# A decode layer on one core: the w2 product in two halves, its weights in runs of 5, 4, 3 and 1 rows, fewer tail DMAs

## The chip, the cores and the metric

The kernel runs on one core of a Trainium2 chip. The metric is the device time of one execution, in microseconds (us). One more number occurs, the *span*, which the profiler measures from the first to the last instruction of one execution; it is about 1.4 us shorter than the time. Engines: PE does matmuls, DVE (VectorE) and ACT (ScalarE) elementwise work, POOL (GpSimd) little here, SP issues loads. The loads run on 16 DMA engines.

Executions of the kernel before lie within about 0.3 us of 661.5 (661.31 to 661.86 in this study); those of some edited kernels spread over about 1 us.

## The reference

```python
h  = x + attention(layernorm(x), k_cache, v_cache, wq, wo)     # B=4, Sq=1, D=640, H=32, Sk=4096, Dh=128
h1 = layernorm(h) @ w1 + b1                                    # w1: 640 x 1728
act = h1 * tanh(softplus(h1))                                  # mish
out = h + act @ w2                                             # w2: 1728 x 640
```

The caches are 268 MB in bf16, the weights 15 MB. All must be read once.

## The kernel before

SP issues every load in order. A loop over 16 tiles of k and v takes the first 624 us. After the last k tile is folded, SP issues the weights of the tail: wo (six DMAs), w1 (three), the last 64 rows of w2 (the *remainder*, since 1728 = 13 x 128 + 64), then the 13 full row groups of w2 (four DMAs). A row group is called a "row" below: 128 rows of w2, one on each partition. Only where the DMAs of the remainder are counted ("eight DMAs of 8 rows") is a row a single row of w2.

```python
WOS = [(k, 0, G) for k in range(NHG - 1)] + [(NHG - 1, a, b) for a, b in ((0, 4), (4, 7), (7, G))]
W1S = (0, 2, DC - 1, DC)                  # w1 in pieces of 2, 2, 1 rows
W2S = tuple(range(0, FM, FI)) + (FM,)     # w2 in runs of 4, 4, 4, 1 rows
# ... cut: sync_prog
for k in range(FT // 8):                  # the remainder: eight DMAs of 8 rows
    r = slice(k // 4 * 32 + k % 4, k // 4 * 32 + 32, 4)
    load(sp, w2_tail[r, :], B_w2[FM * P : F, :][r, :], ("w2t", k), "WT")
sp.need(("PV", NT - 2))
for k, (j0, j1) in enumerate(zip(W2S, W2S[1:])):
    load(sp, w2_sb[:, j0:j1, :], ...)
```

On PE, the tail is one straight program. It adds h1 up as each piece of w1 lands, adds h to the output sum y2, runs four filler matmuls (`busy(4)`, products with zeros whose only use is to keep PE busy), waits for `act`, and adds the w2 rows. The sum y2 has 640 columns for 4 batch rows. It lies in four quarters of 160 columns on PSUM partitions 0, 32, 64, 96, so one w2 row is four matmuls.

```python
# ... cut: pe_tail
for c0, c1 in zip(W1S, W1S[1:]):
    if c1 == DC:
        ...                               # b1 is added before the last piece
    pe.need(("w1", c0))
    for j in [FM] + list(range(FM)):
        for c in range(c0, c1):
            wd = WD if c0 == 0 else 1     # WD = 16: 64 columns on the first piece, 4 on later ones
            mm(h1_w[..., j, 0:wd, :], w, cen[:, c, :]...to_broadcast([P, wd, N]), ...)
...                                       # h into y2: 40 bf16 matmuls (high and low part)
busy(4)
pe.need("act")
def w2_mm(j):
    for k in range(CG):                   # 4 quarters of OC = 160 columns
        mm(y2_ps[k * QD : k * QD + N, :], act[0:rows, j, :], w2_sb[:, j, cs], ...)
pe.need(("w2t", FT // 8 - 1)); w2_mm(FM)
for j0, j1 in zip(W2S, W2S[1:]):
    pe.need(("w2", j0))
    for j in range(j0, j1): w2_mm(j)
```

One DVE copy then takes y2 to SBUF, and four stores (two on the SP queue, two on the ACT queue) write it out.

The softmax here doesn't subtract the row's maximum and nothing guards it: scores larger than these inputs give would overflow.

## Time and profile before

| | before |
|---|---|
| time, median of 6 | 661.53 us (661.38 to 661.82) |
| span of the profiled execution | 660.0 us |
| load queue, share of 16 engines' span | 99.4% |
| PE / DVE busy | 58% / 62% |
| last w2 landing | 657.57 us |

The engine and queue parts of the profile's page, kernel before (busy us, share of the span, instructions; then packets, MB and share of the 16 engines' span):

```profile
PE 383.8 (58%) x2636; PEld 68.4 (10%) x1680; DVE 407.8 (62%) x257; ACT 40.7 (6%) x157; POOL 1.7 (0%) x12
q1 hardware_dynamic: 6912, 283.35, 99.4%
```

No compute engine is near full; the load queue is. The kernel is bound by reading 283 MB, and a change of the tail can only win what lies between the end of the loading and the end of the kernel, or shorten the last loads.

The end of the chain of waits, kernel before (start us, length us, what):

```profile
...
642.29 14.90 DMA slotA<-in_B_w_dram
657.19 0.04 issue
657.23 0.65 PE red L730 x20
657.89 0.02 issue
657.91 0.32 DVE o_bf L726
```

The chain runs through the load of w2 (slotA), then through the last five rows (20 matmuls), then through the copy. PE was waiting for w2.

The timeline of the same end (start, length, engine, line, operation, output<-input, shapes, count, and in brackets the idle time before it and what ended it):

```profile
652.03 0.71 PE L730 MATMUL red<-cen,slotB 128*64 128x4 bf16 x14
...
654.32 0.22 DVE L719 SCALAR_TENSOR_TENSOR act<-tb,hm 128x56 bf16<-128x56 f32 x1
...
654.90 0.30 PE L730 MATMUL red<-w_tail,act 64*4 64x160 bf16 x4
...
655.13 1.27 PE L730 MATMUL red<-slotA,act 128*4 128x160 bf16 x32
...
657.23 0.62 PE L730 MATMUL red<-slotA,act 128*4 128x160 bf16 x20 [0.83 <-DMA slotA<-in_B_w_dram]
657.91 0.32 DVE L726 CAST o_bf<-red 128x160 bf16<-128x160 f32 x1 [3.37 <-PE red L730]
658.26 0.65 SPq L263 DMA_DIRECT2D out_dram<-o_bf  x2
658.27 0.62 ACTq L263 DMA_DIRECT2D out_dram<-o_bf  x2
```

The last w1 matmuls end at 652.7, act is there at 654.5, and PE has 0.83 us of idle time before the last rows. Two stores of each queue take 0.65 us to issue.

### The profile page before, as it was taken

The numbers are of one execution on the slowest core, as the hardware profiler recorded it, in microseconds if no ns is written. First come the engines' busy times: TensorE is split into PE (matmuls) and PEld (weight loads), VectorE is DVE, ScalarE is ACT, GpSimd is POOL, SyncE is SP. The second block draws the span as 40 slices with busy tenths as digits, with TensorE's granted clock in tenths as the row PEclk, the third lists the DMA queues.
The fourth block names the chain that finished last, engine by engine and source line by source line (L and its number), as shares of the span: only waits on it lengthen the run. The fifth ranks groups of instructions, "written<-read, shape, count | busy, mean of one in ns | idle before, by whom it ended". The sixth has DMA issues, their size and how long they took to land. (4 is left out here: it accounts for less than half of the span.)

```text
span 660.0 us, 4989 instructions
## 1 busy us (share of the span) xinstructions
PE 383.8 (58%) x2636; PEld 68.4 (10%) x1680; DVE 407.8 (62%) x257; ACT 40.7 (6%) x157; POOL 1.7 (0%) x12
## 2 busy tenths in 40 slices
PE   1255758457327595838307395838434757665877
PEld 0000100101101010101100010000110001010145
DVE  1087988386048778677219798749206688957612
ACT  0200000000000000000000000000000000000011
POOL 0000000000000000000000000000000000000000
PEclk9778787879659796869668887879876769796868
DMA  9999999999999999999999999999999999999997
GB/s 418 409 445 445 438 441 417 422 441 438 438 437 425 429 437 437 441 437 421 433 437 437 441 437 417 437 437 433 441 441 417 437 433 437 441 441 417 425 416 312
DMA packets 6954, 283.50 MB, mean 430 GB/s; under 512 B 857, under 2 KB 1184, under 8 KB 2208
## 3 DMA queue, kind: packets, MB, share of 16 engines
q1 hardware_dynamic: 6912, 283.35, 99.4%
q8 instruction: 7, 0.11, 0.1%
q14 instruction: 3, 0.02, 0.0%
q10 hardware_dynamic: 32, 0.01, 0.0%
HBM read 283.35 MB, written 0.01 MB: 429 GB/s over the span
## 5 line engine op out<-in xcount | busy, mean ns | idle before, releaser
L529 DVE TENSOR_TENSOR slotA<-slotA,q_bc 128x8192 bf16<-128x8192 bf16 x32 | 140.7, 4416 | 93.1 <-DMA slotA<-in_A_k_cache_dram 93.1
L529 DVE TENSOR_TENSOR slotB<-slotB,q_bc 128x8192 bf16<-128x8192 bf16 x32 | 140.7, 4418 | 18.4 <-DMA slotB<-in_A_k_cache_dram 18.4
L540 DVE TENSOR_REDUCE s_f<-red 128x64 f32<-128x1024 f32 x64 | 78.0, 1219 | 96.3 <-PE red L740 96.2
L740 PE MATMUL red<-slotA,ident 128*128 128x512 bf16 x480 | 135.8, 446 | 0.0
L740 PE MATMUL red<-slotB,ident 128*128 128x512 bf16 x480 | 126.1, 422 | 0.0
L730 PE MATMUL red<-slotA,ident 128*128 128x512 bf16 x32 | 14.7, 458 | 129.4 <-PEq L49 129.4
L730 PE MATMUL pv<-slotC,e 128*32 128x512 bf16 x768 | 51.9, 430 | 37.3 <-PEq L49 34.3
L730 PE MATMUL red<-slotB,ident 128*128 128x512 bf16 x32 | 14.2, 443 | 89.1 <-PEq L49 89.1
L406 ACT ACTIVATE ex<-s_f 128x64 bf16<-128x64 f32 x64 | 16.4, 256 | 513.3 <-DVE s_f L540 513.3
L554 DVE TENSOR_TENSOR e<-ex,hmask 128x512 bf16<-128x512 bf16 x64 | 39.8, 684 | 0.0
L730 PEld LDWEIGHTS pv<-slotC,e 128*32 128x32 bf16 x768 | 22.1, 106 | 95.4 <-issue 81.3
L730 PEld LDWEIGHTS red<-slotA,ident 128*128 128x128 bf16 x32 | 3.2, 99 | 198.0 <-issue 197.9
L730 PEld LDWEIGHTS red<-slotB,ident 128*128 128x128 bf16 x32 | 3.1, 98 | 171.1 <-issue 171.1
L730 PEld LDWEIGHTS o_ps<-pv_sb,selo 128*32 128x32 f32 x136 | 13.5, 109 | 62.6 <-issue 62.6
L730 PE MATMUL o_ps<-pv_sb,selo 128*32 128x128 f32 x136 | 18.0, 276 | 0.0
L730 PE MATMUL pv<-slotA,e 128*32 128x512 bf16 x256 | 14.5, 380 | 0.6 <-PEq L49 0.5
L416 ACT COPY pv_sb<-pv 128x512 f32<-128x512 f32 x16 | 9.4, 586 | 69.5 <-PE pv L730 69.5
L406 ACT ACTIVATION_READ_ACCUMULATOR ex<-s_f 128x1 f32 x64 | 11.9, 186 | 0.0
L730 PEld LDWEIGHTS pv<-slotA,e 128*32 128x32 bf16 x256 | 6.9, 97 | 23.6 <-issue 17.8
L579 DVE RECIPROCAL rl<-misc 32x1 f32<-32x1 f32 x4 | 0.6, 150 | 12.6 <-PE misc L730 12.6
L519 DVE CAST b1T<-pv 128x13 bf16<-128x13 f32 x1 | 0.2, 174 | 12.1 <-PE pv L730 12.1
L730 PE MATMUL y_ps<-a_t,slotB 128*128 128x64 bf16 x160 | 7.3, 211 | 0.0
(107 smaller groups left out, 69.2 us busy)
## 6 DMA issues: line engine op xcount, KB each, us to landing
slotC<-in_A_v_cache_dram SPq DMA_DIRECT2D x2, 4096.0 KB, 42.2
slotC<-in_A_wq_dram SPq DMA_DIRECT2D x1, 5120.0 KB, 15.4
slotB<-in_A_wo_dram SPq DMA_DIRECT2D x3, 1280.0 KB, 15.4
slotA<-in_B_w_dram SPq DMA_DIRECT2D x3, 640.0 KB, 13.9
slotB<-in_B_w_dram SPq DMA_DIRECT2D x2, 864.0 KB, 22.1
slotB<-in_A_wo_dram SPq DMA_DIRECT2D x1, 640.0 KB, 19.0
slotB<-in_A_wo_dram SPq DMA_DIRECT2D x1, 480.0 KB, 19.8
slotB<-in_B_w_dram SPq DMA_DIRECT2D x1, 432.0 KB, 22.8
```

The source lines that it names most:

```text
L406: lambda: a.activation(out=ex[:, sl], in_=s_f[:, sl], func=ACT.Exp, scale=SCALE, accum_out=rs[:, b, s : s + 1],),
L416: lambda: a.copy(out=pv_sb[:, :, :].rearrange("p r d -> p (r d)"), in_=pv[:, :]),
L519: dv.do(lambda: v.tensor_copy(out=b1T[:, 0:FM], in_=b1_ps[:, 0:FM]), "b1m", DV)
L529: lambda: v.tensor_tensor(out=t, in0=t, in1=q_bc[:, hg, b, :].unsqueeze(1).to_broadcast([P, RS, Dh]), op=ALU.mult,),
L540: lambda: v.tensor_reduce(out=s_f[:, s * RS : (s + 1) * RS], in_=red[:, k : k + 2, :].rearrange("p k (r c) -> p (k r) c", c=CW), axis=AX.X ...
L554: lambda: v.tensor_tensor(out=e[:, sl, :], in0=ex[:, sl].unsqueeze(2).to_broadcast([P, RS, G]), in1=hmask[:, :].unsqueeze(1).to_broadcast( ...
L579: dv.do(lambda: v.reciprocal(out=rl[:, :], in_=l_ps), ("rl", hg), DV)
L730: lambda: nc.tensor.matmul(out_, lhsT=lhsT, rhs=rhs, start=start, stop=stop, skip_group_check=skip),
L740: return t.add_instruction(mybir.InstMatmult(name=nc.get_next_instruction_name(), engine=mybir.EngineType.PE, ins=[t.lower_ap(rhs), t.lowe ...
```

## The change

The intent reads from the diff: fewer and larger tail DMAs, two output halves with two copies side by side and one store a queue, and matmuls arranged to keep PE's clock up.

```diff
-    FI = 4
+    FR = (5, 4, 3, 1)                    # w2 runs
-    WOS = ... ((0, 4), (4, 7), (7, G))
-    W1S = (0, 2, DC - 1, DC)
+    WOS = ... ((0, 5), (5, G))
+    W1S = (0, 3, DC)
-        for k in range(FT // 8):
-            r = slice(k // 4 * 32 + k % 4, k // 4 * 32 + 32, 4)
-            load(sp, w2_tail[r, :], B_w2[FM * P : F, :][r, :], ("w2t", k), "WT")
+        load(sp, w2_tail[0:FT, :], B_w2[FM * P : F, :], "w2t", "WT")
 ... cut: stores, one a queue in place of two; b1 in one DMA
+        ac.need(("y2", 1))
+        ac.do(lambda: a.copy(out=o_bf[QD : QD + N, :], in_=y2_ps[QD : QD + N, 1, :]), ("o_bf", 1), "AC")
-        dv.need("y2")
-        dv.do(lambda: v.tensor_copy(out=o_bf[:, :], in_=y2_ps), "o_bf", DV)
+        dv.need(("y2", 0))
+        dv.do(lambda: v.tensor_copy(out=o_bf[0:N, :], in_=y2_ps[0:N, 0, :]), ("o_bf", 0), DV)
 ... cut: weights loaded once for repeated filler matmuls
-                    wd = WD if c0 == 0 else 1
+                    # 64 columns on every piece of w1
-        for part in (h_hi, h_lo):  ...   # 40 bf16 matmuls for h
+        for c in range(DC):  ...         # 10 float32 matmuls for h
-            for k in range(CG):          # 4 quarters of 160 columns
+            for k in range(KO):          # KO = 2 halves of 320 columns
-        for j0, j1 in zip(W2S, W2S[1:]):
+        for j0, j1 in zip(FS, FS[1:]):
+            if j0 == FS[2]:
+                busy(3)                  # called "mid filler" below
             pe.need(("w2", j0))
```

## The prediction

> **What bounds the kernel now.** The page's queue table has the load queue busy 99.4% of 16 engines' span. PE is busy 58% and DVE 62% (engine table). 283.35 MB at about 430 GB/s are almost the whole 660.0 us; the change moves the same bytes, and the attention loop (to about 624 us) is untouched. Only the tail can move.
>
> In the packet records of the tail, the 16 engines do not end together: all are active to about 654.9, half of them at 655.8, three at 656.5, two end at 657.10 and 657.14. The last w2 semaphores are seen about 0.46 us after those packets. From there the exposed chain is (chain of waits, timeline): the last row's four 160-column matmuls to about 657.88, the DVE copy o_bf 657.91 to 658.23 (0.32 us), two store issues on each of two queues 658.26 to 658.91, packets of the second store at 659.4 to 659.5, end 660.0.
>
> **What the change removes.**
> 1. The w2 remainder: eight DMAs of 8 rows become one of 64. The Trainium skill ("DMA: Bandwidth & Descriptors", on how many engines a DMA uses) says that a DMA runs on the largest count up to 16 that divides its outer dimension, the lowest-numbered ones: 8 engines now, 16 after. The two clusters of engine end times, some 0.6 us apart, agree. A 1280-byte packet takes 55 ns and a semaphore packet 9 ns: about 8 x 64 ns now against 4 x 55 + 9 ns on the loaded engines. Estimate: -0.3 us at the stragglers.
> 2. One wo and one w1 DMA less: 16 packets fewer per engine, at about 8 ns overhead each (5120 bytes 196 ns, 6912 262, 10240 385), and two semaphores: -0.15 us.
> 3. One store per queue in place of two: -0.33 us (the second store's packets come 0.35 us after the first's).
>
> **What it adds.** The last row is two matmuls of 320 columns in place of four of 160: +0.1 us. Copies are 320 columns, DVE and ACT in parallel (ACT took 0.59 us for 512 columns, so about 0.45): +0.13 us. The last w1 piece has two rows in place of one, with 64 columns for 4: h1 and act some 0.3 us later. The float32 product of h (10 matmuls for 40) and busy(3) load PE more. These are hidden if PE keeps the full clock. The half clock before, 653 to 657 us (windows view: 0.84, 0.50, 0.80), followed idle PE gaps at 650 to 652; denser w1 work should remove that. The b1 change costs some 0.5 us of PE at 21 us, behind queued K loads: nothing.
>
> **Sum.** -0.3 -0.15 -0.33 +0.1 +0.13 = about -0.55 us. Predicted 661.1 us, range 660.4 to 661.8. Chances: faster by over 2% 0.01, within 2% 0.98, slower 0.01.
>
> **What would show it.** Loop landings unchanged; queue still over 99%; the last w2 packet at about 656.65 instead of 657.14 and engine ends closer together; four single-row packets per engine for the remainder; one store issue of about 0.3 us per queue; copies of 0.4 to 0.5 us on both DVE and ACT; PE waiting for the last w2 DMA, with PE clock near 1.0 from 653 us; act about 655.
>
> **What would make it wrong.** If PE runs at half clock after 653 us, a row of w2 costs about 0.27 us (320 columns, against 0.16 per row read now), and busy(3) over 1.2 us; PE then finishes behind the DMA and the time rises to about 662 or more. Instruction fetches (16 KB packets of 0.95 to 1.2 us, seen at 645.6, 653.1 and 656.8 us) each hold up one engine; shifted code can move one on or off the last engine, worth up to 0.9 us either way. Noise between runs is 0.3 us.

## The result, and the profile after

The changed kernel takes 662.17 us (median of 6, 661.95 to 662.78), the kernel before 661.53. It was 0.64 us slower where 0.4 us faster was predicted (661.1, against the 661.53), and above the predicted range. Ratios are the mean time of one kernel's fast runs over that of the other's in the same rounds, so they are not quite the ratio of the medians quoted: here 1.001, interval 0.9997 to 1.0023. The interval touches 1, but a repetition on another chip gave 662.12 against 661.45, and all 11 executions of the changed kernel (661.95 to 662.93) lie above all those of the kernel before (661.31 to 661.86). The loss is small and real.

The end of the chain of waits, changed kernel:

```profile
...
625.07 27.24 DMA slotB<-in_B_w_dram
652.31 0.04 issue
652.35 2.99 PE red L722 x48
655.34 0.46 PE o_ps L722
655.80 0.65 PE o_ps L732 x3
656.46 1.54 PE red L722 x20
658.00 0.32 PE o_ps L722
658.32 0.44 PE o_ps L732 x2
658.76 0.68 PE red L722 x8
659.44 0.47 DVE o_bf L718
```

The load of w2 is gone from the chain. It now starts with the last piece of **w1** (slotB, landed at 652.31) and then is PE without a gap for 7.1 us. The lines `PE o_ps` are filler: four matmuls before act (655.34 to 656.45) and the three new ones (658.00 to 658.76).

The timeline of the changed kernel, answering the one above:

```profile
652.35 1.83 PE L722 MATMUL red<-cen,slotB 128*64 128x64 bf16 x28 [0.81 <-DMA slotB<-in_B_w_dram]
...
655.76 0.22 DVE L711 SCALAR_TENSOR_TENSOR act<-tb,hm 128x56 bf16<-128x56 f32 x1
...
656.39 0.30 PE L722 MATMUL red<-w_tail,act 64*4 64x320 bf16 x2
...
656.62 1.39 PE L722 MATMUL red<-slotA,act 128*4 128x320 bf16 x18
...
657.93 0.39 PE L722 MATMUL o_ps<-zeros,ident 128*128 128x512 bf16 x1
658.16 0.60 PE L732 MATMUL o_ps<-zeros,ident 128*128 128x512 bf16 x2
...
658.69 0.71 PE L722 MATMUL red<-slotA,act 128*4 128x320 bf16 x8
659.43 0.48 DVE L718 CAST o_bf<-red 4x320 bf16<-4x320 f32 x1 [3.46 <-PE red L722]
659.47 0.42 ACT L441 CAST o_bf<-red 4x320 bf16<-4x320 f32 x1 [4.75 <-PE red L722]
659.91 0.28 ACTq L262 DMA_DIRECT2D out_dram<-o_bf  x1
659.94 0.35 SPq L262 DMA_DIRECT2D out_dram<-o_bf  x1
```

Before, the last rows had a wait in brackets; here they have none. act comes 1.4 us later, and the filler stands between row 9 and row 10. The last w2 packets had landed at 657.53, so PE is about 1.2 us late at the last four rows.

This profiled execution is the slowest of the six (662.78). The windows view shows a likely reason. Lines of the windows 652 to 654 and 654 to 656 us (busy time and instruction count of PE, PEld, DVE, ACT, POOL, then the granted PE clock, the DMA share and GB/s), changed kernel:

```profile
652.00:654.00 2.00, 1.65 (x28) 1.59 (x28) 0.00 (x0) 0.00 (x0) 0.00 (x0) 0.54 1.00 390
654.00:656.00 2.00, 2.00 (x27) 1.07 (x22) 1.53 (x6) 0.25 (x1) 0.00 (x0) 0.60 0.88 351
```

The clock was at half in the w1 stage. A more usual execution (662.02, run a_hbf below, whose only edit does nothing to the time) had full clock there and its act at 655.36; the mid filler still ran from 657.18 on, past the last landing at 657.71, and the last rows began at 657.94. So the half clock is an extra of some executions, and the loss of 0.6 us is there without it.

### The profile page after: what moved, and what is told of

Same layout as the page of the kernel before. It is cut to its first block, busy times and chain, and to the rows that moved or that the text cites. A ratio compares the mean times of both kernels' runs of the same rounds, so it can differ in the third digit from the quotient of the medians.

```text
span 661.3 us, 4896 instructions
## 1 busy us (share of the span) xinstructions
PE 383.9 (58%) x2604; PEld 69.1 (10%) x1631; DVE 407.5 (62%) x255; ACT 41.1 (6%) x158; POOL 1.8 (0%) x13
## 3 DMA queue, kind: packets, MB, share of 16 engines
q1 hardware_dynamic: 6568, 283.35, 99.2%
## 5 line engine op out<-in xcount | busy, mean ns | idle before, releaser
L732 PE MATMUL red<-slotA,ident 128*128 128x512 bf16 x480 | 133.1, 439 | 0.0
L722 PE MATMUL red<-slotA,ident 128*128 128x512 bf16 x32 | 14.5, 452 | 127.4 <-PEq L49 127.4
L722 PE MATMUL red<-slotC,lnT 128*32 128x512 bf16 x40 | 4.5, 630 | 5.4 <-PEq L49 5.4
```

The costliest lines, as they stand in the source:

```text
L722: lambda: nc.tensor.matmul(out_, lhsT=lhsT, rhs=rhs, start=start, stop=stop, skip_group_check=skip),
L732: return t.add_instruction(mybir.InstMatmult(name=nc.get_next_instruction_name(), engine=mybir.EngineType.PE, ins=[t.lower_ap(rhs), t.lowe ...
```

## The experiments

Two theories stood after the comparison. **P:** PE is late, because act comes late, the w2 rows are wider and the mid filler stands in the way; the loads no longer matter. **D:** the end is set by the last w2 landing, which the change failed to move (657.57 before, 657.53 after), and PE's lateness is particular to this trace.

All outputs are right. "a_" kernels are edits of the changed kernel, "b_" kernels of the kernel before. The medians are of five executions (six in the first two rows). Kernels are compared only within the same rounds.

| run | time, us | before | last w1 landing | act starts | last w2 landing | copy starts |
|---|---|---|---|---|---|---|
| before | 661.53 | | 651.91 | 654.32 | 657.57 | 657.91 |
| changed | 662.17 | 661.53 | 652.31 | 655.76 | 657.53 | 659.43 |
| a_nomid | 661.41 | 661.61 | 652.45 | 655.33 | 657.59 | 657.98 |
| a_w1old | 662.81 | 661.61 | 652.52 | 654.86 | 657.75 | 659.47 |
| a_w1old_nomid | 661.52 | 661.61 | 652.25 | 654.61 | 657.45 | 657.85 |
| a_rem8 | 661.65 | 661.61 | 651.95 | 654.83 | 657.62 | 658.23 |
| a_pieces | 661.70 | 661.49 | 652.44 | 654.86 | 657.68 | 658.32 |
| a_cols4 | 663.08 | 661.49 | 652.47 | 655.28 | 657.62 | 659.83 |
| b_rem1 | 661.77 | 661.49 | 652.64 | 654.98 | 657.95 | 658.29 |
| b_halves | 661.57 | 661.49 | 651.89 | 654.37 | 657.54 | 658.05 |
| a_nomid_rem8 | 661.17 | 661.50 | 651.89 | 654.77 | 657.48 | 657.87 |
| a_nomid_rem8_pieces | 661.29 | 661.50 | 651.78 | 654.45 | 657.43 | 657.81 |
| a_nomid_rem16 | 663.38 | 661.50 | 652.12 | 655.00 | 659.22 | 660.14 |
| b_rem4 | 661.55 | 661.50 | 652.90 | 655.23 | 658.01 | 658.34 |
| a_again | 662.12 | 661.45 | 652.27 | 655.64 | 657.50 | 659.58 |
| a_quarters | 661.78 | 661.45 | 652.60 | 655.48 | 657.82 | 658.23 |
| a_hbf | 662.02 | 661.45 | 652.48 | 655.36 | 657.71 | 658.68 |
| best_again | 661.29 | 661.45 | 651.68 | 654.56 | 657.46 | 657.85 |

The times are medians; the four columns on the right are of the one profiled execution (the landings are from the trace's landing records, the last of 16 engines; a landing record is the time at which an engine's notice that its part of a DMA is done reaches the DMA's semaphore). A quick way to read the table is the last column minus the one before it. About 0.4 us means that PE waited for w2. More means that PE was late.

### a_nomid: the mid filler out

```diff
-            if j0 == FS[2]:
-                busy(3)
```

> The changed kernel without the three filler matmuls before the third w2 DMA (busy(3)). Theory P (PE is late): in the changed kernel's trace these ran from 657.93 to 658.76 us while both last w2 DMAs had landed by 657.53, so removing them takes 0.6 to 0.8 us off the time: about 661.5. Theory D (the end is set by when the last w2 packets land, and they land no earlier than before): less than 0.15 us changes. A third possibility: without the filler the clock falls and the last rows run at half speed, which would give part of it back.

It took 661.41 us, 0.20 below the kernel before, where the changed kernel is 0.64 above: the filler costs about 0.8 us. The clock did not fall. Timeline of a_nomid:

```profile
655.33 0.22 DVE L711 SCALAR_TENSOR_TENSOR act<-tb,hm 128x56 bf16<-128x56 f32 x1
...
655.82 2.12 PE L722 MATMUL red<-slotA,act 128*4 128x320 bf16 x26
657.24 0.23 PEld L722 LDWEIGHTS red<-slotA,act 128*4 128x4 bf16 x6 [0.37 <-DMA slotA<-in_B_w_dram]
657.63 0.08 PEld L722 LDWEIGHTS red<-slotA,act 128*4 128x4 bf16 x2 [0.17 <-DMA slotA<-in_B_w_dram]
657.98 0.48 DVE L718 CAST o_bf<-red 4x320 bf16<-4x320 f32 x1 [2.44 <-PE red L722]
```

The waits for w2 (slotA) are back in front of the last rows. Theory D, which allowed 0.15 us, falls. The filler stands in PE's program ahead of its wait for the third w2 DMA, so it runs whether PE has time to spare or not. With act as late as here, PE had none.

### a_w1old, a_pieces and a_cols4: the pieces of w1 and their columns

a_w1old takes both parts back, a_pieces the pieces alone, a_cols4 the columns alone.

```diff
-    W1S = (0, 3, DC)
+    W1S = (0, 2, DC - 1, DC)             # a_w1old, a_pieces
+                    wd = WD if c0 == 0 else 1   # a_w1old, a_cols4: 64 columns on the first piece, 4 later
```

> The changed kernel with w1 in the old pieces of 2, 2 and 1 rows, and 4 columns in place of 64 on the second and third pieces. Theory P: the h1 sum then ends about 1.3 us earlier (652.8 in place of 654.1), act at about 654.7 in place of 656.0, and the time falls by 0.4 to 1.0 us, because PE no longer starts w2 late; the filler still costs. Theory D: act is earlier by as much but the time changes by less than 0.15 us.

> The changed kernel with w1 in the old pieces of 2, 2 and 1 rows, but still 64 columns for every w1 matmul. The run with old pieces and 4 columns came out 0.6 us slower than the changed kernel, with the clock at half from 654.3 to 657.7 us and the 18 w2 matmuls in 2.39 us in place of 1.39. If the columns kept the clock up and the pieces only decide when h1 is done, this run keeps full clock after 652 us, act comes 0.3 to 0.6 us earlier than in the changed kernel, and the time is 661.5 to 661.9. If the pieces themselves cost the clock (a gap between the second and third piece), it is again near 662.8.

> The changed kernel with w1 in the new pieces of 3 and 2 rows, but 4 columns in place of 64 in the second piece. If the columns decide the clock: the half clock falls into the w2 rows again in most executions and the time is 662.3 to 663.0. If the columns do nothing: as the changed kernel, 662.0 to 662.3, or a little less since 28 matmuls of 4 columns are no slower.

a_w1old missed: it was slower, 662.81 us, although act started at 654.86, 0.9 us earlier than in the changed kernel's trace. The two that followed split it. a_pieces (old pieces, 64 columns) took 661.70, which is 0.21 above the kernel before in place of 0.64. a_cols4 (new pieces, 4 columns) took 663.08, four of five executions near 663.1 and one at 661.93. The windows view, a_pieces and then a_cols4:

```profile
654.00:656.00 2.00, 1.78 (x16) 0.43 (x12) 0.98 (x4) 0.00 (x0) 0.00 (x0) 1.00 0.92 369
```

```profile
654.00:656.00 2.00, 2.00 (x18) 0.40 (x7) 1.30 (x5) 0.23 (x1) 0.00 (x0) 0.50 0.89 349
656.00:658.00 2.00, 2.00 (x19) 0.82 (x20) 0.00 (x0) 0.00 (x0) 0.00 (x0) 0.65 0.24 91
```

The clock number (third from the right) is 1.00 with 64 columns and 0.50 with 4. So the columns are a useful part of the change: they cost little (28 matmuls in 1.25 us with 64 columns and in 1.18 with 4 in the traces at full clock) and half clock from the w1 stage on is rarer with them: it starts between 652 and 655 us in two of the eleven traces with 64 columns on every piece (the changed kernel and a_again), and in five of the seven with 4 columns on the later pieces. The pieces of 3 and 2 rows are the harmful part: the last piece leaves 28 matmuls after its landing in place of 14. The fault of a_w1old was to take back both at once.

The Trainium skill ("TensorE: Matmul & The Clock Gate", Part 1) describes two states of the clock and a free-running window of about 3.4 us. The clock records here agree in size: half from 653.37 to 656.79 us in the kernel before, 3.42 us. As the window is not tied to the kernel, executions of one kernel can differ. Whether the one fast execution of a_cols4 is such a case is not shown, since it was not profiled.

### a_w1old_nomid

```diff
+    W1S = (0, 2, DC - 1, DC)             # and 4 columns on later pieces, as a_w1old
-            if j0 == FS[2]:
-                busy(3)
```

> Both: old w1 pieces and no filler before the third w2 DMA. Theory P: PE now waits for the last w2 DMA (landing about 657.5) and the time falls to what my prediction's store and copy terms alone give, 660.9 to 661.2, below the kernel before. Theory D: no change against the changed kernel, about 662.1.

661.52 us: far below the 662.1 of theory D, but a little above the range of theory P. Its trace (full clock, act at 654.61) has PE waiting for w2. Single executions ran from 661.23 to 661.86; with 4 columns the clock is again a matter of chance, but only the first was profiled, so that is not shown for the others.

### a_rem8, b_rem1, b_rem4 and a_nomid_rem16: the remainder of w2

```diff
 # a_rem8 (shown): the changed kernel with eight DMAs of 8 rows; b_rem1: the kernel before with one of 64 rows
 # b_rem4: the kernel before with four of 16 rows; a_nomid_rem16: a_nomid with sixteen of 4 rows
-        load(sp, w2_tail[0:FT, :], B_w2[FM * P : F, :], "w2t", "WT")
+        for k in range(FT // 8):
+            r = slice(k // 4 * 32 + k % 4, k // 4 * 32 + 32, 4)
+            load(sp, w2_tail[r, :], B_w2[FM * P : F, :][r, :], ("w2t", k), "WT")
```

> The changed kernel with the w2 remainder in eight DMAs of 8 rows again. My prediction's step 1 held that eight DMAs load the engines that end last: then the last w2 landing comes 0.3 us later. The rival, from the spread of the per-engine landings (nine engines lead, seven lag by up to 1.7 us already at the last v tile, in both kernels): the eight DMAs of 8 rows put their work on leading engines, so the last w2 landing comes about 0.25 us EARLIER than 657.53 and the landings lie closer together. Under theory P the time itself hardly moves (within 0.15 us), since PE ends the kernel; under theory D it falls by 0.25 us.

> The kernel before with the w2 remainder in one DMA of 64 rows in place of eight of 8: my prediction's step 1 alone. The prediction said -0.3 us. From the first four runs I now expect: last w2 landing within 0.15 us of 657.57; the last w1 landing about 0.4 us later than 651.91 (it came at 652.31 to 652.52 in the three traces with one DMA and at 651.95 with eight); the time unchanged within 0.2 us, because in this kernel PE waits for the last w2 landing and not for act. If instead the time rises by 0.4 us or more, act is on the chain in the kernel before too.

> The kernel before with the remainder in four DMAs of 16 rows, which run on all 16 engines. If what matters is how the rows are spread over the engines, this is like the one DMA: last w2 landing 0.2 to 0.4 us after 657.57, time 661.7 to 661.9. If the number of DMAs or their order against the w1 packets matters, it is like the eight: 661.5, with the last w1 landing near 651.9.

> The changed kernel without the mid filler, remainder in sixteen DMAs of 4 rows, which by the rule of the Trainium skill run on the lowest 4 engines. If the engines that get the extra work are leading ones, as for the eight DMAs the spread of landings suggested for most of them, the other twelve land their last w2 packets about 0.25 us earlier than with one DMA and the time is 661.0 to 661.2. If some of these four are among the lagging ones, they get 0.9 us more work and the last landing and the time move up by 0.5 us or more.

(The rule named in the last text is the one that the prediction cites, with its page.)

The prediction's first step was tested alone in b_rem1, and its sign is wrong: one DMA in place of eight made the kernel before 0.28 us *slower* in the median (661.77 against 661.49; five executions from 661.66 to 661.84 against nine from 661.31 to 661.72), more than the 0.2 us that I had allowed, with the last w2 landing at 657.95. Of the 0.38 us by which this landing is later, 0.15 were there before the tail: the last v landing of the loop came at 624.80 in place of 624.66. Counted from that landing to the last w2 landing, the tail took 32.82 to 32.93 us in the six traces with eight DMAs and 32.86 to 33.15 in the ten with one: 0.1 us more in the mean, and in no case 0.3 less. The landing records of the 16 engines show what the step had overlooked. The v tile that lands last in the loop, kernel before, sorted (us):

```
622.87 622.98 622.99 623.00 623.04 623.09 623.10 623.13 623.16 | 623.48 623.99 624.29 624.50 624.60 624.64 624.66
```

The engines do not come to the tail level. Nine lead, and seven are up to 1.7 us behind. At 53 us 15 of the 16 had landed the second k tile within 0.6 us; by 209 us the nine and the seven had formed, and as the queue is never empty, nobody catches up. The prediction took the two clusters at the end for the work of the eight DMAs. They were there before.

Where the eight DMAs put their rows, only the landings tell, and only by their order, since a record does not name its engine. In a_rem8, four of the leaders advanced by about 1.9 us from the last w1 landing to the first w2 landing, others by about 2.5, and by the same reckoning three of the laggards had the extra work as well. With sixteen DMAs of 4 rows, 15 engines landed their last w2 packets by 657.74 and one alone at 659.22, 1.7 us later than with eight (657.48, a_nomid_rem8), and the time was 663.38. The expectation allowed a lagging engine 0.9 us for its rows, so the rows alone do not account for this, and half clock from 658.90 added to the time. The number of DMAs may count as well as the rows: the last nine of their landing records follow each other at 0.18 us (653.56 to 655.02), as do the last six of the eight DMAs in the kernel before (652.34 to 653.26). Eight more DMAs at 0.18 us are an estimated 1.5 us. This was not tested. Spreading by row count is thus a coarse tool: neither the eight nor the one DMA moved the last landing of the *changed* kernel (657.62 with eight, 657.53 with one).

What the remainder's shape did move, against my expectation that a_rem8 would stay within 0.15 us, is the time: 661.65, 0.04 above the kernel before instead of 0.64. The table's fourth column says how. The last w1 landing was at 651.68 to 651.95 us in all six traces with eight DMAs, at 652.25 to 652.64 in all ten with one, at 652.90 with four and 652.12 with sixteen. In the changed kernel and in a_rem8 the last w1 *packets* end alike (651.57 and 651.58 us), but the landing is recorded 0.74 us after that in one and 0.37 us in the other. The remainder is queued right behind w1, and as one DMA it holds up the notice of w1 by 0.4 us. The same delay, from the last w1 packet to its landing, is 0.32 to 0.46 us in all six traces with eight DMAs, 0.64 to 0.77 in all ten with one, 0.80 with four and 0.56 with sixteen. PE waits for that notice to finish h1, so in the changed kernel, where PE is late, 0.4 us of it are 0.4 us of the time. The remaining 0.2 us of the 0.6 are not accounted for, and why the notice is late was not found.

b_rem4 is inconclusive in its time: 661.55 in the median, but 661.27 to 662.54. Its landings (652.90, 658.01) look like those of one DMA, but its loop had ended late already: the last v landing came at 625.12, and from there to the last w2 landing it took 32.88 us, which lies in both ranges given above. So it does not support the theory of spreading. Only the late notice of w1 is as with one DMA.

### b_halves and a_quarters: the two halves alone, and everything but them

```diff
 # b_halves, on the kernel before; a_quarters is the reverse on the changed kernel
-            for k in range(CG):          # 4 matmuls of 160 columns a row, one copy, two stores a queue
+            for k in range(KO):          # 2 matmuls of 320 columns a row, two copies, one store a queue
```

> The kernel before with only the two w2 halves: two matmuls of 320 columns a row, copies of 320 columns on DVE and ACT side by side, one store a queue. My prediction's step 3 with its additions: -0.33 +0.1 +0.13, about -0.1 us, if PE keeps up (661.4 to 661.6). If the half clock seen after 653 us in the kernel before stays, the two-matmul rows take about 0.27 us each and PE ends its rows 0.3 to 1 us after the last w2 landing: 661.8 to 662.5.

> The changed kernel with the w2 sum in four quarters again (160 columns, one DVE copy, two stores a queue), everything else changed. If the wider rows are what makes PE late, the w2 rows take about half the time (0.87 us for eight rows in the trace of the kernel before with one remainder DMA, 1.39 us for nine rows of halves in the changed kernel), and PE gains about 0.8 us over 14 rows, while the stores lose 0.1: 661.3 to 661.7. If the late act and the filler alone do it, it is 662.0 to 662.4 as the changed kernel.

b_halves took 661.57 against 661.49: nothing, with one execution of five at 662.65. Its last rows took from the landing at 657.54 to 658.05, later than with quarters. a_quarters took 661.78 where a_again, the unchanged changed kernel on the same chip, took 662.12: 0.34 less, although it has the two stores a queue again. That lies between the two ranges of the expectation: the wider rows are a part of the lateness, not all of it. The rows of the run with quarters, and of the usual execution with halves (a_hbf, full clock):

```profile
655.91 1.13 PE L719 MATMUL red<-slotA,act 128*4 128x160 bf16 x36
...
657.73 0.45 PE L719 MATMUL red<-slotA,act 128*4 128x160 bf16 x16
```

```profile
655.86 1.39 PE L732 MATMUL red<-slotA,act 128*4 128x320 bf16 x18
...
657.94 0.71 PE L732 MATMUL red<-slotA,act 128*4 128x320 bf16 x8
```

The first line of each is nine rows, the last is four. Halves take 0.26 us longer on both. The Trainium skill ("TensorE: Matmul & The Clock Gate", Part 3, on packing small matmuls) says that matmuls whose outputs lie in different strips of 32 partitions run side by side; four quarters use four strips and two halves two. The sizes agree in direction: 52 quarters of 13 rows took 1.58 us, 26 halves 2.10 (each the sum of two lines).

### a_hbf: the float32 product of h

```diff
-        for c in range(DC): ...  st[:, c, :], ident_f[...]           # 10 float32 matmuls
+        for part in (h_hi, h_lo): ...  part[:, c, :], ident[...]     # 20 bf16 matmuls
```

> The changed kernel with h added to the w2 sum by bf16 parts again (20 matmuls of 64 columns) in place of 10 float32 ones. These took 0.73 us at full clock and 1.24 us at half, against about 0.9 us for the parts in the kernel before with halves, and they run while act is being computed. Expected: no change, 662.0 to 662.4. If the float32 product is what delays the filler before act and so the first w2 row, 0.2 to 0.4 us less.

662.02 us beside 662.12 for a_again: no effect, as expected.

### a_again, and the best version: a_nomid_rem8, a_nomid_rem8_pieces, best_again

```diff
 # a_nomid_rem8 = best_again: the changed kernel
-            if j0 == FS[2]:
-                busy(3)
 # and the remainder in eight DMAs; a_nomid_rem8_pieces: also W1S = (0, 2, DC - 1, DC), 64 columns
```

> The changed kernel without the mid filler and with the remainder in eight DMAs. Each of the two alone brought it back to 661.4 and 661.65. If both work only by getting PE to the last w2 rows in time, they don't add up: the end is then the last w2 landing (657.5 to 657.7) plus about 2.3 us, 661.2 to 661.5. If the eight DMAs also let the last w2 packets land earlier, it is 661.0 to 661.2.

> The same with the old w1 pieces of 2, 2 and 1 rows and 64 columns throughout. act then comes at about 654.5. If the last w2 landing sets the end, act does not matter any more and the time is that of the run without this step, within 0.15 us, or 0.1 us more for one DMA more. If PE is still late anywhere, another 0.3 us falls away.

> The changed kernel as it is, again, so that it stands beside the other runs of this call on one chip: 662.0 to 662.4, and in the trace PE behind the last w2 landing.

> The best so far again (no mid filler, remainder in eight DMAs), beside the changed kernel on one chip: 661.0 to 661.3, about 1.0 us below the changed kernel and 0.3 us below the kernel before.

The edits do not add up, as expected where all of them only bring PE back in time: 0.8 (filler) and 0.6 (remainder) taken alone, about 1.0 together, and the earlier h1 of the third kernel (act at 654.45) adds nothing: 661.29. a_nomid_rem8 took 661.17 and 661.29, the kernel before 661.50 and 661.45, the changed kernel 662.12 beside the second. The ratio to before is 0.9995 (0.9981 to 1.0009), then 0.9997 (0.9983 to 1.001). It beats the changed kernel by 0.8 us on one chip. Against the kernel before, its ten executions (661.02 to 661.42) lie lower than the 18 beside them (661.33 to 661.81) almost without overlap, but the interval includes 1.

The end of the chain of waits, a_nomid_rem8:

```profile
638.65 18.43 DMA slotA<-in_B_w_dram
657.08 0.04 issue
657.13 0.75 PE red L724 x8
657.88 0.47 DVE o_bf L720
```

The load of w2 heads the chain again, as in the kernel before.

## Why the prediction was wrong, point by point

- **What bounds the kernel: right.** The queue stayed above 99% busy (99.2%), and the median of every variant stayed within 0.3% of 661.5 us.
- **Step 1, the remainder "-0.3 us at the stragglers": wrong, in sign.** Alone on the kernel before it cost +0.28 us in the median (b_rem1). The premise that the eight loaded engines were the ones that ended last came from taking the two clusters of end times as its proof; the clusters are in the landings before the tail begins. A side effect that the prediction didn't have, the notice of w1 0.4 us later, reached the time as well.
- **Step 2, one wo and one w1 DMA less "-0.15 us": not seen on its own.** Steps 1 and 2 together were to bring the last w2 packet to 656.65; it came at 657.13 (657.14 before). One w1 DMA more made no difference that can be told (661.17 and 661.29, last landings 657.48 and 657.43).
- **Step 3 with its additions, "-0.33 +0.1 +0.13": right in size.** From the last w2 landing to the end of the span it is 2.47 us in the kernel before (660.04 - 657.57) and 2.29 us in a_nomid_rem8 (659.77 - 657.48), -0.18 us; in b_halves it is 2.41 us, -0.06. The copies took 0.48 and 0.42 us, the one store about 0.3. But it only counts where PE is on time.
- **"These are hidden if PE keeps the full clock": wrong, and the largest term, +0.8 us.** This overlap is the step that failed most. The prediction named busy(3), the wider rows and the later act, and put them at zero. With full clock (a_hbf) act came at 655.36 rather than 655 and the rows of w2 were still late, since the filler waits for nothing. Adding up the PE lines from the last w1 landing to the last row, as for the chain before, would have shown it: 1.3 us (28 matmuls), 1.8 (to act), 1.6 (remainder and nine rows), 0.8 (filler), 0.7 (four rows) in a_hbf, 6.2 us from 652.5 to 658.7, a full microsecond beyond the last landing.
- **Its warning, half clock after 653 us, "about 662 or more":** the number was met, for the most part by another cause. The two executions of the changed kernel that were seen at half clock (662.78 and 662.93) are 0.7 and 0.8 us above the median of the other nine, which were not profiled.
- **Its other worry, instruction fetches near the end: no effect seen.** The kernel before has a 16 KB fetch at 656.82 us, the changed kernel none after 653.91, and the last w2 landings are 657.57 and 657.53.

The sum: -0.45 us of DMA gain did not come (last landing -0.04), the stores gave about -0.15, and late PE took about +0.8. That is +0.6, and 0.64 was measured.

## What to carry to other kernels

When loads bound a kernel and a short program on PE follows the last of them, add up that program from the *earlier* load it depends on (here w1), not only from the last; slack of 0.8 us is soon spent. Filler matmuls that are meant to hold the clock belong where PE waits anyway: put in the program ahead of a wait, they run whether there is time or not. Before spreading or merging DMAs for balance, read each engine's landings at the start of the stage, since an early lag can last: here the spread of the 16 engines stayed between 1.8 and 2.0 us from 130 to 623 us, under a queue that never emptied.

## What the Trainium skill lacked or had wrong

- "DMA: Bandwidth & Descriptors", Rules for kernel authors, advises to coalesce many small transfers into one large one. Here merging eight DMAs of 10 KB into one of 80 KB made the kernel before 0.28 us slower in the median (b_rem1), and splitting it again made the changed kernel 0.6 us faster relative to the kernel before (a_rem8).
- The same page has nothing on a DMA's completion being noticed later because of the DMA queued behind it: the last w1 landing came 0.64 to 0.77 us after its packets with one remainder DMA behind it (ten traces), and 0.32 to 0.46 us with eight (six traces).
- The same page gives how many engines a DMA uses, which the landing records agree with (72 records for the eight DMAs, nine each: eight engines and one for the rest; 16 for the one). Apart from two engines that it calls usually slower, it does not say that the 16 engines drift apart under a full queue: 1.8 us between first and last landing at 623 us, 0.6 us for 15 of them at 53 us.
- "Runtime: NRT & Kernel Launch", Instruction fetch mechanics, calls the cost of crossing a 16 KiB boundary, for which a block is fetched, mostly hidden. The trace of the kernel before has 16 KB instruction packets of 0.92 to 1.23 us among the packets of the core's DMA engines; four of them and two of 8 KB (0.31 us) fall between 79 and 177 us, when the seven laggards form. That they cause the lag is not shown.
- "TensorE: Matmul & The Clock Gate", the closing table, warns of PE idle gaps over about 3 us. In a_cols4 no gap between PE's matmuls in the window ahead of 653.97 us was over 0.9 us, and the clock fell to half there; with 64 columns in place of 4 and gaps of that size (a_pieces) it held. For the shorter idles that the page also mentions it gives no length.
